# Merged weight words of block 0: from PSUM banks to a buffer in SBUF

## The chip, the cores and the metric

The kernel runs on one core of one Trainium2 chip. The metric is the device time of one execution in microseconds (us). Before the change it is 1144.56 us, the median of 3 runs (1143.82 to 1144.73).

Engines are named as in the profile: PE is TensorE's matmul side and PEld its weight load, DVE is VectorE, ACT is ScalarE, POOL is GpSimd, SP is the queue that issues the DMAs.

## The reference

`x` is 4 x 4096 x 192, `weight_gen` 4 x 4096 x 8 x 7, `w_in` 192 x 2048, `w_out` 2048 x 192, all fp32.

```python
w = softmax(weight_gen)                      # over the last axis, 7 taps
x_pad = concat(zeros(B, 6, D), x)            # causal, along the sequence
out[b, s, h, :] = sum_k w[b, s, h, k] * x_pad[b, s + k, h, :]   # 8 heads of 24
h = out.reshape(16384, 192) @ w_in
g = where(h >= 1, h, where(h <= -1, 0, (h + 1)**2 / 4))
return g @ w_out                             # 16384 x 192
```

## The kernel before

The 16384 tokens are cut into 32 blocks of 512. For each block the dynamic convolution runs on POOL (7 products and 6 sums of 128 x 768, lines 171 to 202), the result is transposed, and two matmuls follow: gemm1 (192 to 2048, line 378) and gemm2 (2048 to 192, line 432). To keep fp32 accuracy each operand is split into a high part in TensorE's fp32r form and a low rest: gemm1 has three passes (high x high, low weight x high, high weight x low) over three pieces of the contraction, 9 passes on each of two row halves, 18 matmuls for a pair of hidden chunks. gemm2 has 32 matmuls for a pair. A block has 16 steps (hidden chunks of 128), that is 8 pairs; there are 256 pairs in all. Between gemm1 and gemm2 stand, for each step, relu and square on ACT (lines 389 and 392), act_g on DVE (397), and the split into gh on ACT (403) and gl on DVE (404).

The order on every engine is the order in which the program is written (`manual_schedule`): each engine takes its instructions one by one. The loop over pairs w (line 676) writes gemm1 of pair w, then gemm2 of pair w - 2, then the elementwise work of pair w; `side` holds work for other blocks that is put into places of this loop.

Block 0 is special: while its pairs run, the weights are decoded, one chunk c (of 8) ahead of the pair that uses it. A chunk has two parts, part 0 for `w_in` and part 1 for `w_out`. For each part:

- cast: the top halves of the raw words go to a 16-bit head, on ACT (`cast_act`, line 327) or DVE (`cast_dve`, line 331);
- `merge(c, part)` (line 340, DVE): a shift-and-or of two SBUF operands, 128 x 384 words, makes the value that the fp32r copy is to see; its output `psw` is a tile of the PSUM pool `ps_h`;
- `high(c, part)` (line 352, ACT): copies `psw` to whi or wo;
- `low(c, part)` (line 356, DVE): `psw` less the high part, into wlo or the low half of wo.

`ps_h` has four banks under one tag. In block 0 they are shared by the two `psh` tiles of gemm1 of a pair, by the two `psw` tiles of a chunk, and by the `psx` tiles of the transposes of blocks 0 and 1. A tile takes the bank that was freed first; so gemm1 of pair w writes the banks that low(w, 0) and low(w, 1) have just freed, and its first two matmuls wait for these two instructions.

`early_pair(w)` (line 631) writes for pairs 2 to 6: merge(c, 0), merge(c, 1) with c = w + 1, one operation of block 1's convolution on POOL, relu of step 2w, high(c, 0), high(c, 1), low(c, 0), low(c, 1), square, relu, square, act_g, the next chunk's cast on DVE, a second operation on POOL, act_g, the splits, the next chunk's cast on ACT. `first_pairs` (line 589) does the same for pairs 0 and 1 and chunks 1 and 2, with one softmax product (line 155) and three convolution products on POOL behind merges. In block 0 each POOL operation has an added dependency (`held`, line 191) on the last merge or cast on DVE that is written ahead of it ("the decoding of a chunk goes first"). After chunk 7 POOL has the last two sums of block 1's convolution; their result is copied in part by ACT (`again`), transposed on TensorE (`turn1`), split by ACT and DVE (`edge_pair`, line 656), and is what gemm1 of pair 8, the first of block 1, needs.

`XT` is the SBUF tile (128 x 3 x 4 x 128 fp32, one buffer) into which the transposed rows of a block are gathered by DMA, from block 2 on (`transpose_out`, line 271). Block 2's gather is the first to write it.

Of the kernel before, what the change touches and what calls it, by code (L numbers as in the profile page):

```python
# [10 lines left out]
F32 = mybir.dt.float32  # L11
# [11 lines left out]
def kernel(  # L23
# [22 lines left out]
    P = 128  # L46
# [33 lines left out]
    xt = ctx.enter_context(tc.tile_pool(name="xt", bufs=2))  # L80
# [5 lines left out]
    ps_h = ctx.enter_context(tc.tile_pool(name="ps_h", bufs=4, space=bass.MemoryType.PSUM))  # L86
# [211 lines left out]
    C1 = NC * P  # L298
# [31 lines left out]
        o, i = tops(c, part)  # L330
        marks.append(nc.vector.tensor_scalar(out=o, in0=i, scalar1=0.5, scalar2=None, op0=ALU.mult))  # L331

    psw = {}

    def merge(c, part):
        word = raw_t[c].bitcast(U32)[:, 1:1 + 2 * CN].rearrange("p (c t) -> p c t", t=2)[:, :, 0]
        upper = heads[c % 2].rearrange("p c t -> p (c t)").bitcast(U32)
        psw[c, part] = ps_h.tile([P, 512], F32, tag="h", name="psw")
        sl = (slice(0, C1), slice(C1, CN))[part]
        marks.append(nc.vector.scalar_tensor_tensor(  # L340
            out=psw[c, part].bitcast(U32)[:, 0:sl.stop - sl.start], in0=word[:, sl], scalar=13, in1=upper[:, sl],
            op0=ALU.logical_shift_right, op1=ALU.bitwise_or))
# [190 lines left out]
    with tc.manual_schedule():  # L533
# [31 lines left out]
        for k, t in enumerate(pieces):  # L565
            for c in range(NC):
                turn_sum(src, t, k == 0, k == len(pieces) - 1, c)
        merge(0, 0)
        cast_dve(0, 1)
        high(0, 0)  # L570
        run(s1[4:6])
        low(0, 0)
        run(split_x(0, src, [nc.vector] * NC))
        cast_dve(1, 2)
        merge(1, 0)
        turned1 = whole()
        n_ops = conv(1, nc.gpsimd, marks, turned1)
# [10 lines left out]

        def first_pairs():
            merge(0, 1)  # L590
            merge(1, 1)
            tc.add_manual_dep(s1[6]().ins, marks[-1].ins.name, SYNC, reason="the decoding of a chunk goes first")
# [159 lines left out]
```

## Time and profile before

| what | value |
|---|---|
| median of 3 runs | 1144.56 us (1143.82 to 1144.73) |
| the profiled execution, its own time | 1144.88 us |
| its span | 1142.4 us |
| PE busy | 1128.4 us (99%) |
| PEld busy | 1112.8 us (97%) |
| ACT busy | 964.5 us (84%) |
| DVE busy | 834.3 us (73%) |
| POOL busy | 792.4 us (69%) |
| mean granted TensorE clock | 0.997 |
| chain that ended last | PE 96% (gemm1 49%, gemm2 46%) |

Times in the rows are counted from the span's start. The span is what the profile covers of the execution; the execution's own time is 2.5 us longer. Busy shares are means over the whole span; block 0, which the change touches, takes the first 60 us of it, and for that stretch the rows by window and the instruction lists are read instead. In an instruction list "x2" means two instructions of one kind in a row, and an entry in brackets the idle time before it and what ended it.

### The profile page before, as it was taken

The page shows a single profiled execution, that of the slowest core. Times are in us where ns is not written, and L with a number is a line of the kernel's source. Part 1 is how long each engine was busy: PE and PEld are TensorE (multiplying, and loading weights), DVE is VectorE, ACT ScalarE, POOL GpSimd, SP SyncE. Part 2 cuts the span into 40 slices and gives each one's busy share as a digit, 9 for nine tenths or more (in the row PEclk, how much of TensorE's full clock was granted, in tenths as well). Part 3 has the DMA queues.
Part 4 walks back from the last instruction along what each step waited for, and adds up shares of the span by engine and source line. Part 5 has one row for each costly group of instructions (what it writes and reads, how often), then busy time and mean ns, then how long its engine had stood idle before and what let it go on. Part 6 is the DMA issues. An engine that isn't in the chain of part 4 may idle for free.

```text
span 1142.4 us, 32241 instructions
## 1 busy us (share of the span) xinstructions
PE 1128.4 (99%) x12885; PEld 1112.8 (97%) x12885; DVE 834.3 (73%) x1271; ACT 964.5 (84%) x1745; POOL 792.4 (69%) x511
## 2 busy tenths in 40 slices
PE   7999999999999999999999999999999999999998
PEld 5889999999999999999999999999999999999998
DVE  8887867777676777767777677776767777677765
ACT  6878888888888888888888888888888888888886
POOL 4699876777857678486686866778576785866310
PEclk9899999999999999999999999999999999999999
DMA  9512222222222122222122222222222122221100
GB/s 230 116 67 83 92 85 92 72 64 79 90 78 91 59 74 89 73 96 90 44 90 73 86 91 78 65 73 90 77 92 72 61 91 82 81 91 43 48 24 29
DMA packets 84053, 91.43 MB, mean 80 GB/s; under 512 B 5056, under 2 KB 75712, under 8 KB 83904
## 3 DMA queue, kind: packets, MB, share of 16 engines
q1 hardware_dynamic: 83904, 89.39, 24.6%
q8 instruction: 101, 1.65, 0.6%
q14 instruction: 48, 0.39, 0.1%
HBM read 64.99 MB, written 24.38 MB: 78 GB/s over the span
## 4 chain that ended last, share of the span: by engine, by line
PE 96%; ACT 1%; DVE 1%; DMA 0%; POOL 0%; issue 0%; SPq 0%; DVEq 0%; POOLq 0%
PE psh L378 49%; PE o L432 46%; PE psx L267 1%; DMA x<-in_x_dram 0%; ACT u L392 0%; ACT u L389 0%; ACT gh L403 0%; DVE psh L397 0%; DVE psw L340 0%; ACT whi L352 0%; POOL piece L189 0%; POOL acc L189 0%; ACT wo L352 0%; DVE gl L404 0%; DVE wo L356 0%
## 5 line engine op out<-in xcount | busy, mean ns | idle before, releaser
L432 PE MATMUL o<-wo,gh 64*128 64x384 f32 x4096 | 638.3, 353 | 1.0 <-SPq L441 1.0
L432 PE MATMUL o<-wo,gl 64*128 64x192 f32 x4096 | 615.1, 247 | 0.0
L432 PEld LDWEIGHTS o<-wo,gh 64*128 64x128 f32 x4096 | 609.3, 184 | 2.4 <-SPq L441 1.2
L432 PEld LDWEIGHTS o<-wo,gl 64*128 64x128 f32 x4096 | 591.3, 188 | 0.7
L397 DVE SCALAR_TENSOR_TENSOR psh<-u,psh 128x512 f32<-128x512 f32 x512 | 354.4, 695 | 282.2 <-ACT u L392 281.8
L378 PE MATMUL psh<-hc,whi 64*128 64x512 f32 x1536 | 436.6, 396 | 3.6 <-DVE wlo L356 2.5
L378 PE MATMUL psh<-hc,wlo 64*128 64x512 f32 x1536 | 430.5, 389 | 0.0
L378 PE MATMUL psh<-hl,whi 64*128 64x512 f32 x1536 | 429.5, 388 | 0.0
L389 ACT ACTIVATE u<-psh 128x512 f32<-128x512 f32 x512 | 301.4, 589 | 79.0 <-PE psh L378 77.8
L404 DVE TENSOR_TENSOR gl<-psh,gh 128x512 fp32r<-128x512 f32 x512 | 345.2, 684 | 15.5 <-ACT gh L403 1.1
L403 ACT ACTIVATE gh<-psh 128x512 fp32r<-128x512 f32 x512 | 299.0, 591 | 64.7 <-DVE psh L397 64.7
L189 POOL TENSOR_TENSOR acc<-acc,pr 128x768 f32<-128x768 f32 x185 | 343.4, 1856 | 6.5 <-DVE head L331 2.8
L392 ACT ACTIVATE u<-u 128x512 f32<-128x512 f32 x512 | 324.3, 633 | 16.0
L179 POOL TENSOR_TENSOR pr<-x,w 128x768 f32<-128x768 f32 x186 | 286.6, 1548 | 7.0 <-DVE psw L340 7.0
L378 PEld LDWEIGHTS psh<-hc,whi 64*128 64x128 f32 x1536 | 270.6, 185 | 8.7 <-DVE wlo L356 3.9
L378 PEld LDWEIGHTS psh<-hl,whi 64*128 64x128 f32 x1536 | 270.5, 185 | 3.1 <-DVE hl L259 0.3
L378 PEld LDWEIGHTS psh<-hc,wlo 64*128 64x128 f32 x1536 | 270.9, 186 | 1.6
L259 POOL TENSOR_TENSOR hl<-XT,hc 128x512 fp32r<-128x512 f32 x90 | 115.8, 1303 | 206.9 <-PE o L432 151.6
L179 POOL TENSOR_TENSOR acc<-x,w 128x768 f32<-128x768 f32 x31 | 47.9, 1546 | 70.2 <-DVE w L155 68.3
L258 ACT ACTIVATE hc<-XT 128x512 fp32r<-128x512 f32 x90 | 55.5, 618 | 0.0
L284 DVE STREAM_TRANSPOSE T<-acc 128x768 f32<-128x768 f32 x30 | 50.2, 1672 | 0.0
L457 DVE SCALAR_TENSOR_TENSOR osb<-o,osb 128x384 f32<-128x384 f32 x64 | 32.5, 548 | 2.8 <-ACT osb L456 2.8
(44 smaller groups left out, 188.8 us busy)
## 6 DMA issues: line engine op xcount, KB each, us to landing
x<-in_x_dram SPq DMA_DIRECT2D x28, 960.0 KB, 5.0
XT<-D SPq DMA_DIRECT2D x180, 128.0 KB, 2.7
out_dram<-osb SPq DMA_DIRECT2D x31, 384.0 KB, 3.1
D<-T SPq DMA_DIRECT2D x30, 384.0 KB, 2.3
x<-in_x_dram SPq DMA_DIRECT2D x4, 945.0 KB
w<-in_weight_gen_dram SPq DMA_DIRECT2D x15, 224.0 KB, 2.6
r<-in_moe_w_in_dram SPq DMA_DIRECT2D x16, 192.0 KB, 7.3
r<-in_moe_w_out_dram SPq DMA_DIRECT2D x8, 384.0 KB, 12.5
```

What stands on the lines that cost most here:

```text
L179: held(eng.tensor_tensor(out=t, in0=xtile[:, k:k + n, :].rearrange("p j (h g) -> p j h g", h=H), in1=wt[:, gi, :, :, k:k + 1].to_broadcast ...
L189: held(eng.tensor_tensor(out=o, in0=s, in1=t, op=ALU.add))
L258: ops.append(lambda c=c: nc.scalar.activation(out=hc[:, c], in_=src[c], func=AF.Copy))
L259: ops.append(lambda c=c: lows.append(engines[c].tensor_tensor(out=hl[:, c], in0=src[c], in1=hc[:, c].bitcast(F32), op=ALU.subtract)))
L284: lambda: nc.vector.transpose(out=T.rearrange("p b c j -> p b j c"), in_=acc.rearrange("p j (r b) -> p b j r", b=R)),
L378: nc.tensor.matmul(out=pair[h][:, 0:N], lhsT=l[rows, f // 2, (c + h) % NC if b < 2 else c], rhs=r[rows, c], start=(s == 0), stop=(s == len ...
L389: nc.scalar.activation(out=u_t[i], in_=h_t[i][:, 0:N], func=AF.Relu, scale=0.5 * UNIT, bias=0.5)
L392: nc.scalar.activation(out=u_t[i], in_=u_t[i], func=AF.Square, scale=UNIT ** -0.5)
L397: nc.vector.scalar_tensor_tensor(out=pv, in0=uv, scalar=1.0 / UNIT, in1=pv, op0=ALU.min, op1=ALU.max)
L403: nc.scalar.activation(out=gh[:, 0:N], in_=gv, func=AF.Copy)
L404: nc.vector.tensor_tensor(out=gl[:, 0:N], in0=gv, in1=gh[:, 0:N].bitcast(F32), op=ALU.subtract)
L432: mm = nc.tensor.matmul(out=o_t[b][turn][:, k, 0:cols], lhsT=g_t[i][l][rows, t * P:(t + 1) * P], rhs=wo[rows, f].rearrange("p s d -> p (s ...
```

## The change

The words that merge makes no longer stand in PSUM. One SBUF tile of four quarters (128 x 4 x 384 fp32) is taken from the buffer `XT`, which is not in use before block 2; a chunk's part takes the quarter 2 * part + c % 2. The PSUM banks of `ps_h` are left to `psh` and `psx`. Who writes and reads the words stays: merge on DVE writes, high on ACT and low on DVE read. The order of the instructions stays too.

```diff
-    psw = {}
+    psw, words = {}, []
 
     def merge(c, part):
         word = raw_t[c].bitcast(U32)[:, 1:1 + 2 * CN].rearrange("p (c t) -> p c t", t=2)[:, :, 0]
         upper = heads[c % 2].rearrange("p c t -> p (c t)").bitcast(U32)
-        psw[c, part] = ps_h.tile([P, 512], F32, tag="h", name="psw")
+        if not words:
+            words.append(xt.tile([P, 4, C1], F32, tag="XT", name="words", bufs=1))
+        psw[c, part] = words[0][:, 2 * part + c % 2]
         sl = (slice(0, C1), slice(C1, CN))[part]
         marks.append(nc.vector.scalar_tensor_tensor(
             out=psw[c, part].bitcast(U32)[:, 0:sl.stop - sl.start], in0=word[:, sl], scalar=13, in1=upper[:, sl],
```

## Rows read from the trace of the kernel before

**Rows 1.** Busy us (and instructions) by stretch; PEclk is the granted clock's share.
```profile
core 0: us, PE busy (x) PEld busy (x) DVE busy (x) ACT busy (x) POOL busy (x), PEclk, DMA share, GB/s
12.00:60.00 48.00, 42.49 (x380) 35.21 (x380) 42.85 (x80) 40.30 (x79) 27.75 (x18) 0.93 0.68 156
...
60.00:1135.00 1075.00, 1075.00 (x12428) 1069.79 (x12428) 780.36 (x1176) 919.25 (x1656) 757.09 (x481) 1.00 0.23 76
```

**Rows 2.** Chain of waits in order of time: start us, us, what.
```profile
30.16 4.57 PE psh L378 x18
...
59.99 2.07 PE psh L378 x18
62.05 2.25 PE o L432 x32
```

**Rows 3.** ScalarE's instructions, pair 4: start us, us, what, idle before.
```profile
39.87 0.60 ACT L389 ACTIVATE u<-psh 128x512 f32<-128x512 f32 x1 [0.49 <-PE psh L378]
```

**Rows 4.** VectorE's instructions from chunk 6's merges to chunk 7's.
```profile
44.89 1.02 DVE L340 SCALAR_TENSOR_TENSOR psw<-r,head 128x384 uint32<-128x384 uint32 x2
46.01 0.56 DVE L356 TENSOR_TENSOR wlo<-psw,whi 128x384 fp32r<-128x384 f32 x1
46.48 0.55 DVE L356 TENSOR_TENSOR wo<-psw,wo 128x384 fp32r<-128x384 f32 x1
...
48.75 1.45 DVE L404 TENSOR_TENSOR gl<-psh,gh 128x512 fp32r<-128x512 f32 x2
50.11 1.02 DVE L340 SCALAR_TENSOR_TENSOR psw<-r,head 128x384 uint32<-128x384 uint32 x2
```

**Rows 5.** POOL's instructions, pair 5 to the end of block 1's convolution.
```profile
46.06 1.55 POOL L179 TENSOR_TENSOR pr<-x,w 128x768 f32<-128x768 f32 x1 [1.33 <-DVE psw L340]
...
51.28 1.83 POOL L189 TENSOR_TENSOR acc<-acc,pr 128x768 f32<-128x768 f32 x1 [1.37 <-ACT whi L352]
53.19 1.85 POOL L189 TENSOR_TENSOR piece<-acc,pr 128x768 f32<-128x768 f32 x1
```

**Rows 6.** All engines in order of time, 114 to 118 us.
```profile
114.20 1.56 POOL L179 TENSOR_TENSOR pr<-x,w 128x768 f32<-128x768 f32 x1
...
114.56 1.68 DVE L150 TENSOR_TENSOR w<-w,m 128x448 f32<-128x448 f32 x1
...
115.70 2.25 POOL L189 TENSOR_TENSOR acc<-acc,pr 128x768 f32<-128x768 f32 x1
```

**Rows 7.** Two lines of the softmax: ns min/median/max over the trace, forms.
```profile
L150 DVE TENSOR_TENSOR w<-w,m x16: 381/615/1676, 3.2 to 1014.2; 128x448 f32<-128x448 f32 x14, 128x224 f32<-128x224 f32 x2
...
L153 DVE TENSOR_SCALAR s<-s x17: 185/904/1801, 5.0 to 1028.1; 128x64 f32<-128x64 f32 x15, 128x32 f32<-128x32 f32 x2
```

**Rows 8.** All engines in order of time, chunks 1 to 3.
```profile
18.88 0.55 DVE L356 TENSOR_TENSOR wlo<-psw,whi 128x384 fp32r<-128x384 f32 x1
...
19.11 0.98 POOL L155 TENSOR_TENSOR w<-w,s 128x448 f32<-128x448 f32 x1 [7.11 <-DVE psw L340]
...
19.55 1.02 DVE L356 TENSOR_TENSOR wo<-psw,wo 128x384 fp32r<-128x384 f32 x2
...
21.92 1.54 POOL L179 TENSOR_TENSOR acc<-x,w 128x768 f32<-128x768 f32 x1 [1.83 <-DVE psw L340]
...
22.77 0.54 DVE L356 TENSOR_TENSOR wo<-psw,wo 128x384 fp32r<-128x384 f32 x1
...
23.42 3.05 POOL L179 TENSOR_TENSOR pr<-x,w 128x768 f32<-128x768 f32 x2
...
28.42 0.57 DVE L340 SCALAR_TENSOR_TENSOR psw<-r,head 128x384 uint32<-128x384 uint32 x1
```

**Rows 9.** ScalarE's groups by form, hc: busy us, mean ns, idle before.
```profile
L258 ACT ACTIVATE hc<-XT 128x512 fp32r<-128x512 f32 x90 | 55.5, 618 | 0.0
...
L258 ACT ACTIVATE hc<-psx 128x512 fp32r<-128x512 f32 x6 | 3.2, 594 | 0.4 <-PE psx L267 0.3
```

**Rows 10.** Busy us by stretch, columns as in rows 1, around the low clock.
```profile
26.80:30.16 3.36, 1.42 (x18) 1.17 (x17) 3.20 (x8) 2.81 (x7) 0.63 (x1) 0.94 1.11 209
29.74:36.57 6.83, 6.41 (x35) 5.48 (x37) 5.81 (x12) 5.60 (x12) 4.72 (x3) 0.50 1.11 216
```

## The prediction

> **What bounds the kernel now.** Read the stretches by engine first [rows 1]: from 60 to 1135 us TensorE is busy 1075.00 of 1075.00 us at the full clock, so nothing done there by another engine is worth anything, and any delay of the point where this stretch begins is a delay of the end, one for one. The change touches only block 0, which is over at 60 us. In 12 to 60 TensorE has 5.5 us of idle and runs below full clock, while VectorE and ScalarE are busy 43 and 40 of 48 us; so the question is what decides when TensorE's closed stretch begins, at 59.8 us.
>
> The chain of waits [rows 2] shows it: it goes through TensorE only where the clock was low (4.57 us for the 18 matmuls of pair 3, against 2.07 for the same 18 at 59.99), otherwise it hops between VectorE and ScalarE. One pair on VectorE [rows 4]: two merges at T = 44.89, two low() at 46.01 and 46.48, two act_g, a cast, two gl from 48.75, and the next merges at 50.11. That is 5.22 us with hardly a gap. Four such intervals from merge(3,0) at 28.42 to merge(7,0) at 50.11 make 5.42 each [rows 4, 8]. Beside it POOL runs block 1's conv, each operation released by a merge or a cast [rows 5]: the product at 46.06 lasts 1.55 us and lies across both low().
>
> **What the change removes.** The first pass of gemm1_pair(w) no longer takes the banks that low(w, 0) and low(w, 1) free, so it can start behind high(w, 0). That is worth at most one low() per pair (0.55 us) and only where TensorE is late. ScalarE waited 0.49 us for gemm1 of pair 4 at 39.87 [rows 3]; in pairs 5 and 6 it didn't wait for TensorE at all. So the gain is at most 0.5 us, and nothing if something else gets later. I take 0.
>
> **Durations of the moved operands.** high() now reads SBUF: hc from XT takes 618 ns, from PSUM 594, at 512 columns [rows 9], so 0.02 to 0.04 us more; one of them lies on the path in each of seven chunks, +0.2 us. merge() and low() on VectorE: a sum of two SBUF operands takes 615 ns at 448 columns and 381 at 224 [rows 7], that is 1.04 ns a column and 0.55 us at 384, which is what low() takes now with one operand in PSUM [rows 4]. So 0 there. SP's queue gets no new instruction; a weight load waits for the merges four chunks ahead of its own, so it shifts as they do and stays as far ahead of its use.
> [...]
>
> **What the change adds: low() reads two SBUF operands.** The case in the trace that decides is a TENSOR_TENSOR on VectorE with both operands in SBUF while POOL works [rows 6]: POOL's product runs 114.20 to 115.76; VectorE's operation began at 114.56 and took 1.68 us, ending at 116.24, 0.48 behind POOL. The same operation takes 0.615 in the median [rows 7]. POOL's next one then took 2.25 in place of 1.85 and ended 1.71 behind VectorE's. So one waits for the other, in turn, and who waited ends at the other's end plus its own duration less 0.13. low() of today, with one operand in PSUM, takes its 0.55 under POOL's product without any stretch [rows 4, 5].
> [...]
>
> So a low() ends 0.42 us after POOL's operation, a product (1.55) 1.42 and an add (1.85) 1.72 after VectorE's. Four terms.
>
> *Chunks 0 and 1* [rows 8]. low(1,0) runs from 18.88 to 19.43 and holds POOL's softmax product: this one, ready at 19.11 (0.98), ends at 19.43 + 0.85 = 20.28; low(0,1) ends at 20.70 where it ended at 20.10. VectorE has no idle there: **+0.6**.
>
> *Chunk 2* [rows 8]. Behind merge(2,1) POOL has three products queued, the first from 21.92, now 22.52 to 24.07. low(2,0) waits for it: ends 24.49. Product 2 is waiting then and goes next, to 25.91; low(2,1) ends at 26.33 instead of 23.32, 3.0 later. Before merge(3,0) lie three act_g, four gl and a cast, 7 x 0.60 + 0.29 = 4.5 us with some 0.2 of waiting (5.1 in the trace, which held 0.5 of idle that is gone, since ScalarE has caught up): merge(3,0) at 31.0, not 28.42. So 2.6 in all, **+2.0** beyond the first term.
>
> *Pairs 2 to 5.* From T: low(c,0) T+1.14 to T+1.69, just ahead of POOL's product (T+1.17, as 46.01 against 46.06); POOL goes next, to T+3.11; low(c,1) to T+3.53; then act_g, cast, act_g and gl (2.1), a wait of 0.1 for gh, gl (0.6): next merge at T+6.27 against 5.42. If POOL comes first, the two low() end at T+3.6, which is the same. 4 x 0.85 = **+3.4**.
>
> *Chunk 7* [rows 5]. POOL's last two operations are adds and the end of block 0 hangs on them. Before: 53.19 + 1.85 - 50.11 = T+4.93. Now low(7,0) to 1.70, add to 3.42, low(7,1) to 3.84, last add to 5.56: **+0.6**. From there again(), the transposes and the split are what they were.
>
> Sum 6.6, with the 0.2 of high() 6.8 us.
>
> **TensorE's clock.** [...] I take a fifth, 0.6 us. Low end 0, high end 3.4.
>
> **The sum.** The profiled execution took 1144.88 us (span 1142.4), 0.3 above the median of 1144.56. 1144.88 + 6.8 + 0.6 = 1152.3; against the median 1152.0 us.
>
> **Rivals.**
> [...]
> 2. The clock falls in the last idle: 6.8 + 3.4 to 4: 1155 us. For it: gemm1 of pair 7 is done near T+3.8 and the transposes start behind the last add and again(), near T+6.1, an idle of 2.3 us. Against: before the end it fell only once in the trace, and about as long an idle is then spread over every pair.
> 3. The other side: low() isn't blocked, because what blocked at 114.56 was the broadcast operand or the softmax's layout, not the second SBUF operand. Then only the freed banks count: gemm1 of pair 3, at 30.16, starts one low() earlier, behind high(); pairs 3 and 4 move up by 0.55, of which ScalarE's wait of 0.49 lets 0.5 through [rows 2, 3]: 1144.1 us, up to 0.7 less if the low clock is missed too. The point that decides is whether low() keeps 0.55 us under a POOL operation. [...]
> 4. The change doesn't free what it says, since the words' buffer makes a new wait: merge(c+2) into the same quarter, or block 2's gather into XT. Neither is late: low(c) is ahead of merge(c+2) on VectorE itself, and block 2's gather is written into the order six turns of the pair loop behind low(7,1). Price 0, so it only joins rival 3.
>
> **Chances.** The forecast 0.55, rival 1 0.17, rival 2 0.18, rivals 3 and 4 0.10. A difference under 0.2% (2.3 us) can't be told from none. Forecast, rivals 1 and 2 are slower by more: 0.89 with a little of rival 1's low end taken off; same 0.09; faster 0.02. The range leaves out rival 3 and the far end of rival 2: 1147.5 to 1156.5 us.
>
> **What would show it.** low() (L356) with a mean over 1 us, the longest 1.5 or more, each ending some 0.4 us behind a POOL operation; POOL's products in block 0 at over 1.9; the merges of chunk 7 at about 56 us and the closed stretch of TensorE from about 67; high() at 0.51. [...] The prediction is wrong if low() stays at 0.55 under POOL, or if the stretch up to the merges of chunk 7 grows by less than 3 us.

## The result, and the profile after

The changed kernel takes 1151.3 us in the median of six runs (1149.89 to 1152.16), the kernel before beside it 1144.29: a ratio of 1.0055 [1.004, 1.007]. That is slower by 0.55%, as forecast, 0.7 us under the predicted time and inside its range. The profiled execution took 1150.63 us with a span of 1148.8, against 1144.88 and 1142.4.

Busy time by stretch, after, answers to [rows 1]:

```profile
core 0: us, PE busy (x) PEld busy (x) DVE busy (x) ACT busy (x) POOL busy (x), PEclk, DMA share, GB/s
12.00:66.00 54.00, 41.11 (x373) 32.86 (x373) 51.01 (x79) 40.77 (x79) 29.55 (x18) 0.94 0.61 139
...
32.90:39.73 6.83, 5.91 (x34) 5.12 (x36) 6.08 (x10) 4.84 (x10) 3.84 (x3) 0.50 0.87 173
...
66.00:1141.00 1075.00, 1075.00 (x12428) 1069.77 (x12427) 780.94 (x1175) 919.34 (x1657) 757.33 (x481) 1.00 0.23 76
```

The closed stretch of TensorE is the same 1075 us with the same 12428 matmuls; it begins 6 us later. The clock's half stretch lies at 32.9 to 39.7, where it began at 29.7. In front of the closed stretch ScalarE does the same 79 instructions in the same 40 us, and VectorE is busy 51.0 us for 79 instructions where it was 42.9 for 80. With no instruction added, the 8.2 us more are time in which the engine stands inside an instruction. Which one, the groups of instructions say (ns min/median/max of the eight of each part, first and last start):

```profile
L358 DVE TENSOR_TENSOR wlo<-words,whi x8: 494/558/1916, 14.1 to 57.1; 128x384 fp32r<-128x384 f32 x8
L358 DVE TENSOR_TENSOR wo<-words,wo x8: 545/1474/2201, 19.3 to 57.5; 128x384 fp32r<-128x384 f32 x8
```

L358 is low(), L356 before (the lines behind merge() stand two further down). Eight of its sixteen instances keep their 0.49 to 0.56 us; the others take 1.05 to 2.20, and the mean of all is 1.15. What holds them stands on POOL. VectorE, chunks 2 and 3, then from chunk 6's merges to the end of chunk 7 (start, us), as [rows 4, 8]:

```profile
20.98 1.01 DVE L342 SCALAR_TENSOR_TENSOR words<-r,head 128x384 uint32<-128x384 uint32 x2
22.50 1.69 DVE L358 TENSOR_TENSOR wlo<-words,whi 128x384 fp32r<-128x384 f32 x1
24.12 1.90 DVE L358 TENSOR_TENSOR wo<-words,wo 128x384 fp32r<-128x384 f32 x1
...
30.71 1.02 DVE L342 SCALAR_TENSOR_TENSOR words<-r,head 128x384 uint32<-128x384 uint32 x2
...
49.64 1.02 DVE L342 SCALAR_TENSOR_TENSOR words<-r,head 128x384 uint32<-128x384 uint32 x2
50.78 0.56 DVE L358 TENSOR_TENSOR wlo<-words,whi 128x384 fp32r<-128x384 f32 x1
51.25 1.90 DVE L358 TENSOR_TENSOR wo<-words,wo 128x384 fp32r<-128x384 f32 x1
...
55.92 1.02 DVE L342 SCALAR_TENSOR_TENSOR words<-r,head 128x384 uint32<-128x384 uint32 x2
...
57.53 2.20 DVE L358 TENSOR_TENSOR wo<-words,wo 128x384 fp32r<-128x384 f32 x1
```

and POOL beside it, as [rows 5]:

```profile
18.74 1.16 POOL L155 TENSOR_TENSOR w<-w,s 128x448 f32<-128x448 f32 x1 [7.08 <-DVE words L342]
...
22.24 1.54 POOL L179 TENSOR_TENSOR acc<-x,w 128x768 f32<-128x768 f32 x1 [2.34 <-DMA x<-in_x_dram]
23.74 3.67 POOL L179 TENSOR_TENSOR pr<-x,w 128x768 f32<-128x768 f32 x2
...
50.80 1.94 POOL L179 TENSOR_TENSOR pr<-x,w 128x768 f32<-128x768 f32 x1 [1.10 <-DVE words L342]
...
57.08 2.24 POOL L189 TENSOR_TENSOR acc<-acc,pr 128x768 f32<-128x768 f32 x1 [1.10 <-ACT whi L354]
59.40 2.01 POOL L189 TENSOR_TENSOR piece<-acc,pr 128x768 f32<-128x768 f32 x1
```

Pair 6 shows the turns. low(6,0) starts at 50.78, 0.02 us ahead of POOL's product, and keeps its 0.56. The product takes 1.94 where it took 1.55 and ends at 52.74; low(6,1), issued at 51.25, ends at 53.15, 0.41 behind it. In chunk 2 POOL's product has begun at 22.24 before low(2,0), and low(2,0) ends at 24.19, 0.41 behind its end; the next product, the first of the two in the row of 23.74, goes before low(2,1) and ends at 25.60, and low(2,1) ends only at 26.02. All eight stretched low() of this trace end 0.41 to 0.42 behind the end of a POOL operation.

The chain of waits now (start, us), as [rows 2]:

```profile
31.85 1.93 DVE wlo L358
...
33.82 3.83 PE psh L380 x12
...
38.68 1.44 DVE wlo L358
...
51.34 1.61 DVE wo L358
...
57.61 1.62 DVE wo L358
...
66.37 2.08 PE psh L380 x18
```

In every chunk from 3 on a stretched low() is a link of the chain: in chunks 3 and 4, where POOL's product had begun first, it is low(c,0), from chunk 5 on low(c,1). The same 18 matmuls that open the closed stretch begin at 66.37 instead of 59.99.

### The profile page after: what moved, and what is told of

It is laid out like the page before. It is cut to its first block, busy times and chain, and to the rows that moved or that the text cites. A ratio compares the mean times of both kernels' runs of the same rounds, so it can differ in the third digit from the quotient of the medians.

```text
span 1148.8 us, 32234 instructions
## 1 busy us (share of the span) xinstructions
PE 1127.7 (98%) x12885; PEld 1111.1 (97%) x12885; DVE 843.7 (73%) x1271; ACT 965.5 (84%) x1745; POOL 794.4 (69%) x511
## 4 chain that ended last, share of the span: by engine, by line
PE 95%; DVE 3%; ACT 1%; issue 0%; DMA 0%; DVEq 0%; SPq 0%
PE psh L380 49%; PE o L434 46%; DVE wo L358 1%; PE psx L267 1%; DVE wlo L358 1%; DVE psh L399 1%; ACT gh L405 0%; DVE words L342 0%; DMA w<-in_weight_gen_dram 0%; ACT whi L354 0%; ACT u L391 0%; DVE head L331 0%; DVE gl L406 0%; DVE piece L227 0%; DVE s L153 0%
## 5 line engine op out<-in xcount | busy, mean ns | idle before, releaser
L434 PEld LDWEIGHTS o<-wo,gh 64*128 64x128 f32 x4096 | 602.6, 184 | 2.5 <-DVE gl L406 1.3
L380 PE MATMUL psh<-hc,whi 64*128 64x512 f32 x1536 | 424.8, 396 | 6.4 <-ACT whi L354 6.4
L380 PE MATMUL psh<-hc,wlo 64*128 64x512 f32 x1536 | 420.3, 390 | 3.5 <-DVE wlo L358 3.3
L380 PE MATMUL psh<-hl,whi 64*128 64x512 f32 x1536 | 419.2, 388 | 0.0
L380 PEld LDWEIGHTS psh<-hc,whi 64*128 64x128 f32 x1536 | 261.5, 185 | 10.2 <-ACT whi L354 7.9
L380 PEld LDWEIGHTS psh<-hc,wlo 64*128 64x128 f32 x1536 | 262.2, 186 | 7.1 <-DVE wlo L358 5.1
L380 PEld LDWEIGHTS psh<-hl,whi 64*128 64x128 f32 x1536 | 261.3, 185 | 3.0 <-DVE hl L259 0.3
```

The source lines that it names most:

```text
L380: nc.tensor.matmul(out=pair[h][:, 0:N], lhsT=l[rows, f // 2, (c + h) % NC if b < 2 else c], rhs=r[rows, c], start=(s == 0), stop=(s == len ...
L434: mm = nc.tensor.matmul(out=o_t[b][turn][:, k, 0:cols], lhsT=g_t[i][l][rows, t * P:(t + 1) * P], rhs=wo[rows, f].rearrange("p s d -> p (s ...
```

## The experiments

Two measures are taken from every profile. "Block 0" is the time from the start of low(1,0) to the first matmul of pair 8: 40.94 us before, 47.70 after; it leaves out the arrival of the first transfers. "Last interval" is from chunk 6's merges to chunk 7's: 5.22 before, 6.28 after; no trace has a stretch of half clock in it (granted clock 1.00 from 36.57 to 60.00 before, from 39.73 to 66.00 after). Times are medians, but of one execution each where a kernel was run once more; the kernel before beside them lay at 1143.9 to 1144.3.

| kernel | time, us | block 0, us | last interval, us |
|---|---|---|---|
| before / after | 1144.3 / 1151.3 | 40.94 / 47.70 | 5.22 / 6.28 |
| part 0's words alone in SBUF, two traces | 1146.41; 1147.66 | 42.28; 42.75 | 5.23; 5.22 |
| part 1's words alone in SBUF, two traces | 1147.6; 1146.41 | 43.49; 43.47 | 5.89; 5.89 |
| POOL held behind both low() | 1148.38 | 45.70 | 5.97 |
| the same, and the cast ahead | 1147.89 | 46.08 | 5.59 |
| POOL only writes: after / before | 1143.45 / 1143.3 | 40.38 / 40.18 | 5.24 / 5.22 |
| POOL in halves: after / before | 1148.18 / 1144.0 | 44.64 / 40.36 | 5.76 / 5.23 |
| after, once more | 1152.16 | 48.90 | 6.28 |

Block 0 isn't free of the clock. In the trace before, half clock from 29.7 to 36.6 us (0.50 in [rows 10]) lengthened two intervals, by 0.8 us in all. And from the end of POOL's last add to pair 8 it takes 4.8 us in every trace in which POOL does the convolution, except three with half clock in just this stretch: POOL held (5.7 us, half clock from 59.4 to 62.8; mean granted clock of the execution 0.998), the same with the cast ahead (5.7; 60.5 to 63.9; 0.995) and the changed kernel once more (6.2; 63.4 to 66.8; 0.995).

**Half of the change: part 0's words, or part 1's.** Part 1's differs in the number alone.

```diff
-        psw[c, part] = words[0][:, 2 * part + c % 2]
+        psw[c, part] = words[0][:, 2 * part + c % 2] if part == 0 else ps_h.tile([P, 512], F32, tag="h", name="psw")
```

> Words of part 0 (w_in) alone stand in SBUF, those of part 1 are back in PSUM. Theory (low() with two SBUF operands and POOL's operation wait for each other in turn): low(c,0) mostly starts just ahead of POOL's operation, so it keeps 0.55 us in most chunks and POOL's product is stretched instead (1.9 us); low(c,1), in PSUM, is never stretched. So about 1.1 us over the kernel before, near 1145.4 (1144.5 to 1147). Rival A (a word in SBUF costs by itself, whoever else works): half of the whole change's 6.4, near 1147.5, with low(c,0) long in every chunk. Rival B (what costs is that gemm1 runs into other banks): the same as the whole change as soon as a bank is freed, near 1150.

> Words of part 1 (w_out) alone stand in SBUF, those of part 0 are back in PSUM. Theory: low(c,1) comes when POOL's operation is running in every chunk, ends 0.42 behind it (about 1.4 us long), low(c,0) keeps 0.55. About 3.6 us over the kernel before, near 1147.9 (1146.8 to 1149): three times as much as with part 0 alone. Rival A: the same as part 0 alone, near 1147.5. Rival B: the same as part 0 alone, near 1150.

Part 0's: 1146.41 us (1145.59 to 1154.57), 1.0026 [1.0014, 1.0038]; block 0 +1.34. Part 1's: 1147.6 us, 1.0028 [1.0017, 1.0039]; block 0 +2.55. The low() of the part that stayed in PSUM keeps 0.55 us in both, and the one with two SBUF operands is the one that waits (it takes up to 1.92 us for part 0, 1.80 for part 1). But part 1 costs about twice part 0 by block 0, not three times; the two intervals of the ratio overlap, so the times alone don't tell the halves apart. The longest of the first runs of part 0, which is the one that was traced, had something else in it (last section). So both were run once more.

> Words of part 0 alone in SBUF once more, for a trace without the 6.9 us that VectorE stood at 117 us in the first one. Theory: 1 to 1.6 us more than the kernel before between low(1,0) and pair 8; the softmax subtraction at 117 us waits for one POOL operation (1.5 to 1.8 us) as in the other traces, or again for all that POOL has queued.

> Words of part 1 alone in SBUF once more, for a trace without the late first transfers of the first one. Theory: 2.5 to 3.5 us more than the kernel before between low(1,0) and pair 8, low(c,0) at 0.55 and low(c,1) at 1.4 to 1.5 in every chunk from 3 on.

Part 0 again: 1147.66 us, block 0 +1.81, somewhat over the 1 to 1.6 expected; part 1 again: 1146.41, +2.53, with low(c,1) at 1.44 to 1.51 in chunks 3 to 6 and at 1.80 in chunk 7, where POOL's operation is an add. VectorE with part 1 alone, chunk 6:

```profile
46.60 0.55 DVE L342 SCALAR_TENSOR_TENSOR words<-r,head 128x384 uint32<-128x384 uint32 x1
47.25 0.56 DVE L358 TENSOR_TENSOR wlo<-psw,whi 128x384 fp32r<-128x384 f32 x1
47.74 1.51 DVE L358 TENSOR_TENSOR wo<-words,wo 128x384 fp32r<-128x384 f32 x1
```

POOL beside it:

```profile
47.30 1.54 POOL L179 TENSOR_TENSOR pr<-x,w 128x768 f32<-128x768 f32 x1 [1.09 <-DVE words L342]
```

The product lies across both low(). It neither holds nor is held by the first, which reads PSUM, and keeps 1.54 us; the second ends 0.41 behind it. Now part 0 alone, VectorE in chunks 3 and 6:

```profile
29.84 1.92 DVE L358 TENSOR_TENSOR wlo<-words,whi 128x384 fp32r<-128x384 f32 x1
31.68 0.55 DVE L358 TENSOR_TENSOR wo<-psw,wo 128x384 fp32r<-128x384 f32 x1
...
47.70 0.56 DVE L358 TENSOR_TENSOR wlo<-words,whi 128x384 fp32r<-128x384 f32 x1
...
49.26 0.65 DVE L331 TENSOR_SCALAR head<-r 128x384 f16<-128x384 bf16 x1
```

and POOL:

```profile
29.80 1.54 POOL L179 TENSOR_TENSOR pr<-x,w 128x768 f32<-128x768 f32 x1 [1.90 <-DVE psw L342]
...
47.73 1.94 POOL L179 TENSOR_TENSOR pr<-x,w 128x768 f32<-128x768 f32 x1 [1.10 <-DVE psw L342]
```

Here a lead of 0.03 us decides. In chunk 6 low() is ahead (47.70 against 47.73): POOL waits, its product ends at 49.67, the cast waits a little (0.65 for 0.38), and the interval is 5.22 us, as before the change. In chunk 3 POOL is ahead (29.80 against 29.84) and low() takes 1.92; that interval is 6.29 in both traces of this kernel. This lost start alone lengthens one interval by 1.07, where 1.1 us had been expected for all of block 0. The waiting cast costs nothing here. The second trace has one more long interval, 6.36 behind chunk 4's merges, which begins at half clock (mean of this execution 0.997) and has a low(4,0) of 0.96, behind 1.14 us of waiting for high().

The two halves don't add up to the whole: 3.9 to 4.3 us against 6.76 by block 0. That gap is too wide, because the 0.8 us of half clock in the trace before is taken off each half; by the medians it is 2.2 + 3.4 against 7.0. The last interval, free of the clock, shows it best: 0.01 for part 0 and 0.67 for part 1, but 1.06 for both. The rows say why: with part 1 alone low(c,1) waits 0.96 us (1.51 - 0.55), because the product had started unhindered. With both, the first low() pushes the product back by 0.4 and the second low() waits for the pushed product, 1.35 (1.90 - 0.55). A conflict that costs nothing by itself makes the next one longer, here by 0.39.

**POOL held behind both low().** POOL's first operation of a chunk is written behind low(c,1) and waits for it, so that neither low() can meet one.

```diff
-        nc.vector.tensor_tensor(out=lo, in0=src, in1=hi.bitcast(F32), op=ALU.subtract)
+        marks.append(nc.vector.tensor_tensor(out=lo, in0=src, in1=hi.bitcast(F32), op=ALU.subtract))
...
-            wave(1)
             if c + 4 < NCH:
...
             low(c, 1)
+            wave(1)
```

> The changed kernel with POOL's first operation of a chunk (three in chunk 2) written behind both low() and made to wait for the second one, not for the second merge. Theory: every low() is back at 0.55 us, but POOL's product now lies over the cast on DVE, which waits for it (over 1 us), and the following add runs into the next merges; about 1.6 us less than the changed kernel, 4.7 over before, near 1149.1 (1147.5 to 1150.5). Rival A: low() as long as in the changed kernel (mean 1.15 us), and later POOL work: 1151 or more. Rival B: as the changed kernel, 1151.

Measured 1148.38 us, 1.004 [1.0028, 1.0052]; block 0 45.70. VectorE in chunk 6:

```profile
47.71 0.56 DVE L358 TENSOR_TENSOR wlo<-words,whi 128x384 fp32r<-128x384 f32 x1
48.18 0.55 DVE L358 TENSOR_TENSOR wo<-words,wo 128x384 fp32r<-128x384 f32 x1
...
49.30 1.37 DVE L331 TENSOR_SCALAR head<-r 128x384 f16<-128x384 bf16 x1
```

POOL:

```profile
48.88 1.55 POOL L179 TENSOR_TENSOR pr<-x,w 128x768 f32<-128x768 f32 x1 [2.24 <-DVE wo L358]
```

Both low() are back at 0.55, and so is every other but low(0,1), which still meets the softmax product (1.05). The wait has moved to the cast: 1.37 us, ending 0.24 behind the product. Here VectorE goes first with both low() and the cast then waits, at an interval of 5.97; left to themselves, the two engines didn't take turns that way. Of the 45.70 some 0.9 us is the clock just before pair 8 (see above).

**The same, with the cast in front.** As the last, and the cast goes behind the merges, where POOL is still in its add.

```diff
             merge(c, 1)
-            wave(1)
+            if c + 1 < NCH:
+                cast_dve(c + 1, 1)
...
             low(c, 1)
+            wave(1)
...
-            if c + 1 < NCH:
-                cast_dve(c + 1, 1)
```

> As the kernel that holds POOL behind both low(), and the cast on DVE is written ahead of them, behind the merges, so that POOL's two operations of a chunk follow each other and only the next chunk's first merge can wait. Theory: low() 0.55, cast 0.38, one merge of a chunk stretched; about 3.3 us over before, near 1147.6 (1146.3 to 1149), 1.4 less than with the cast where it was. Rival A: no less than the changed kernel. Rival B: as the changed kernel, 1151.

Measured 1147.89 us, 1.0035 [1.0023, 1.0047]. VectorE:

```profile
47.09 1.36 DVE L342 SCALAR_TENSOR_TENSOR words<-r,head 128x384 uint32<-128x384 uint32 x2
...
52.68 0.89 DVE L342 SCALAR_TENSOR_TENSOR words<-r,head 128x384 uint32<-128x384 uint32 x1
```

and POOL's add, under which the merge of 52.68 begins:

```profile
51.30 1.85 POOL L189 TENSOR_TENSOR acc<-acc,pr 128x768 f32<-128x768 f32 x1
```

The casts are at 0.38 and both low() at 0.55. Now the first merge, which reads two SBUF operands too, takes 0.89 instead of 0.55, ending 0.42 behind the add. The last interval is 0.4 shorter than with the gate alone, yet block 0 is no shorter, 46.08 against 45.70, and the medians differ by 0.5 us where 1.4 was expected. Both traces lost 0.9 us to the clock just before pair 8, so that isn't the difference. But in this one the clock was at half from 29.8 to 36.6 us as well (mean granted clock 0.995, where it was 0.998 with the gate alone), and the first two intervals took 6.58 and 6.06 where the last two took 5.6; how much of that is the clock was not separated. In all three places that were tried for POOL's work in this loop, some VectorE instruction with SBUF operands meets it (a low() of 1.90 us, a cast of 1.37, a merge of 0.89).

**POOL only writes.** POOL's 13 products and sums of block 1 become memsets of the same tiles under the same gates, in the changed kernel and in the one before. Shown is the cut at the sums; the products have the same.

```diff
-            held(eng.tensor_tensor(out=o, in0=s, in1=t, op=ALU.add))
+            if gate:
+                held(eng.memset(o, 0.0))
+            else:
+                eng.tensor_tensor(out=o, in0=s, in1=t, op=ALU.add)
```

> The changed kernel with POOL's 13 operations of block 1's convolution replaced by memsets of the same tiles, which write SBUF and read nothing (block 1's convolution is left out, its softmax product on POOL stays). Theory (the conflict is over reads): low() is back at 0.55 us from chunk 2 on; only the softmax product still holds low(0,1) of chunks 0 and 1 (0.5 us). So within 0.3 to 1.2 us of the kernel before with the same memsets, near 1144.6. Rival A (a word in SBUF costs by itself): 6 us over the kernel before with the same memsets, low() with a mean of 1.15. If a POOL write alone conflicts too, low(c,1) is stretched by up to the memset's length, some 2 us in all.

> The kernel before with the same memsets in place of POOL's 13 operations of block 1's convolution (left out in the same way). All theories: the kernel's VectorE and ScalarE chain in block 0 stays, POOL's last two operations are shorter, so 0.2 to 1 us below the kernel before, near 1143.8. It is the base for the changed kernel with memsets.

Measured 1143.45 us for the changed kernel, 1.000 [0.999, 1.001] of the unedited kernel before, and 1143.3 for the other, 0.9993 [0.9984, 1.0001]. The 6.8 us are gone but for 0.15 us in the medians and 0.2 in block 0, less than the expected 0.3 to 1.2. The 0.2 is made of 0.56 that low(0,1) still waits for the softmax product (1.05 us), 0.03 in an interval (5.25 against 5.22), and some 0.5 the other way, which the second kernel's trace lost to half clock (16 matmuls of gemm1 took 3.86 us at 30.55, and two intervals 5.39 and 5.56 for 5.22). VectorE in the changed one (low() is L364 there):

```profile
46.03 0.56 DVE L364 TENSOR_TENSOR wlo<-words,whi 128x384 fp32r<-128x384 f32 x1
46.51 0.56 DVE L364 TENSOR_TENSOR wo<-words,wo 128x384 fp32r<-128x384 f32 x1
...
47.63 0.40 DVE L337 TENSOR_SCALAR head<-r 128x384 f16<-128x384 bf16 x1
```

and POOL:

```profile
45.97 0.74 POOL L180 MEMSET pr<- 128x768 f32 x1 [2.34 <-DVE words L348]
```

low() starts under POOL's memset and takes its 0.56, where one under the product took 1.90. So words in SBUF cost next to nothing by themselves, 0.15 us in the medians, which rules out every explanation by their place alone (longer instructions, a wait for the buffer, the order on the engines), and a memset, the one POOL instruction here that only writes SBUF, holds nobody: in these runs the conflict comes with POOL's reads.

**POOL in halves.** Each of the 13 operations is cut into two of 128x384, in both kernels. Shown is the cut at the sums; the products have the same.

```diff
-            held(eng.tensor_tensor(out=o, in0=s, in1=t, op=ALU.add))
+            for j in parts:
+                held(eng.tensor_tensor(out=o[:, j], in0=s[:, j], in1=t[:, j], op=ALU.add))
```

> The changed kernel with each of POOL's 13 operations of block 1's convolution cut into two of half the columns (128x384). Theory: a low() waits for one POOL instruction, now about 0.9 us long, so no low() is over 1.5 us (1.9 to 2.2 before the cut) and the intervals between merges shrink from 6.3 to about 5.8: 2.9 us less than the changed kernel, near 1148.4 (1147 to 1150). Rival A: the length of POOL's instructions doesn't matter, 1151. Rival B: 1151.

> The kernel before with the same cut of POOL's operations. All theories: no low() is stretched; POOL's two operations of a chunk get 0.2 us longer each and the last adds end later: 0.3 us over the kernel before (0 to 1), near 1144.6. It is the base for the cut in the changed kernel.

Measured 1148.18 us, 1.0038 [1.0026, 1.005], and 1144.0, 1.0001 [0.9992, 1.001]. VectorE in the changed kernel (low() is L361):

```profile
47.97 0.56 DVE L361 TENSOR_TENSOR wlo<-words,whi 128x384 fp32r<-128x384 f32 x1
48.44 1.22 DVE L361 TENSOR_TENSOR wo<-words,wo 128x384 fp32r<-128x384 f32 x1
```

and POOL:

```profile
47.99 2.40 POOL L180 TENSOR_TENSOR pr<-x,w 128x384 f32<-128x384 f32 x2 [1.03 <-DVE words L345]
```

low(6,1) now ends at 49.66, inside POOL's two halves (47.99 to 50.39): it goes in between them and waits for one half instead of the whole, 0.67 us instead of 1.35. Halving POOL's instructions takes 3.1 of the 6.8 us away, at no cost to the kernel before, whose low() doesn't wait at all. The price of the change thus goes with the length of the other engine's instruction.

**The changed kernel once more.**

> The changed kernel once more, for a second trace. Theory: from low(1,0) to the first matmul of pair 8 it takes 47.7 us as in the first trace (40.9 in the kernel before), give or take 0.7 with where TensorE's clock falls; of two low() of a chunk one is stretched, by one POOL operation. Rival: the clock carries a good part of the loss; then a trace with the clock elsewhere differs by 2 us or more in that stretch.

1152.16 us, block 0 48.90, 1.2 more than in the first trace: outside the 0.7 that was allowed, and short of the rival's 2. Again one low() of each chunk from 3 on is stretched, and the last interval is the same 6.28; the difference is at the end of block 0, where it takes 6.2 us from POOL's last add to pair 8 instead of 4.8. Busy time by stretch in this second trace:

```profile
core 0: us, PE busy (x) PEld busy (x) DVE busy (x) ACT busy (x) POOL busy (x), PEclk, DMA share, GB/s
60.00:68.00 8.00, 5.92 (x46) 4.84 (x46) 5.61 (x10) 5.64 (x11) 8.00 (x5) 0.79 0.00 0
63.40:66.80 3.40, 3.40 (x21) 2.81 (x20) 2.48 (x4) 2.03 (x5) 3.40 (x3) 0.50 0.00 0
```

From 63.4 to 66.8 the clock was at half (0.50), and in this stretch lie the last gemm2 and transposes on which pair 8 waits. In the first trace it was at full speed there and had fallen from 32.9 to 39.7, inside block 0, where ScalarE once waited 0.75 us for gemm1 and the intervals stayed at 6.29 to 6.35.

No variant that does all of the work beat the kernel before. The only part of the change that can gain, the freed banks, stays under the 0.5 us of the prediction: with POOL's reads gone from block 1's convolution the changed kernel isn't faster than the kernel before edited in the same way.

## Why the prediction was right

Step by step, in its own terms. All of the changed trace up to chunk 1 lies 0.37 us earlier, since the first x transfer landed earlier (POOL's wait for it ended at 7.11 us, before at 7.46); this is taken out below.

| step | forecast | measured |
|---|---|---|
| chunks 0 and 1: merge(2,0) later by | 0.6 | 20.98 for 20.76: 0.59 |
| chunk 2: merge(3,0) later by, in all | 2.6 | 30.71 for 28.42: 2.66 |
| interval of pairs 2 to 5 | 6.27 for 5.42 | 6.30; four make 3.5 |
| merges of chunk 7 at | about 56 | 55.92 |
| chunk 7: POOL's last add ends, from its merges | 5.56 for 4.93 | 5.49 |
| high() | 0.51 | 0.51 to 0.53 |
| mean of low(), longest | over 1, 1.5 or more | 1.15, 2.20 |
| low(1,0) to pair 8 | +6.8 | +6.76 |

**What carried it.** One stretched instruction elsewhere in the trace [rows 6], together with the observation that today's low() is not stretched [rows 4, 5], gave the rule (two SBUF operands wait, in turn, and end 0.42 behind) and the price. All eight stretched low() end 0.41 to 0.42 behind a POOL operation, as forecast. The merges and low() themselves are as long as they were (0.550 us for a merge that writes SBUF, 0.559 before). So the trace shows 9 ns less for a merge and nothing for a low() that doesn't wait.

**The interval's 0.88 is two things.** Free of half clock the interval went from 5.22 to 6.29, 1.07 more. Before, the stretch of half clock made two intervals 5.84 and 5.41, 0.8 us lost; after, a fall of the same 6.83 us cost next to nothing, since TensorE had idle to spare: it was busy 5.91 us of it, where it was 6.41 before. 4 x 1.07 - 0.8 = 3.5. The forecast set its 6.27 against a mean that half clock had lengthened and came out right, since the fall inside block 0 cost next to nothing, but the conflict alone is dearer than its 0.85.

**Where the sum was lucky.** 6.8 against 6.76 is closer than the working deserves. The addends of the interval, 3.53 + 2.1 + 0.1 + 0.6, make 6.33 as they stand and not 6.27, and high()'s 0.02 was in its T+1.14 already, so the 0.2 added for high() at the end counts it a second time for most chunks. The four terms, forecast at 6.6, measured 0.59 + 2.07 + 3.52 + 0.56 = 6.74 with high() in them; the extra 0.2 happened to fill what they were short of. A fifth of 3.4 for the clock is 0.7, not 0.6.

**Where the numbers part.** The profiled execution was forecast at 1152.3 and took 1150.63. The 1.65 us between are: 0.6 for the clock at the end of block 0, which this execution didn't spend; 0.37 for the early start; 0.04 in block 0; and 0.65 outside the span (1.83 us there, 2.48 before; 1.86 in the second trace of the changed kernel). The last stays unexplained. The clock term was the author's estimate, a fifth of a high end of 3.4, and no run shows a loss of either size. What the runs show is a matter of chance: the second trace lost 1.4 us at the end of block 0, the first nothing, and the runs lie between 1149.9 and 1152.2. The high end was too high: where the clock fell in the last idle it cost 0.9 to 1.4 us (POOL held, the same with the cast ahead, the changed kernel once more), and each of these stretches of half clock is 3.4 us long, where the one in [rows 10] took 6.83.

**The rivals.** As in the sum, POOL got its turn between two low() that stood in a row (50.80 between 50.78 and 51.25); VectorE went first with both only where POOL was held back by hand. Rival 3 fell with low() at 1.90 and with a cast without broadcast that took 1.37 us for 0.38 under POOL's product, and the gain that it named doesn't show even where nothing blocks: with memsets an interval is 5.25 against 5.22. Its bound of 0.5 us passed over ScalarE's wait for gemm1 of pair 3, 0.92 us at 34.45 in the trace before. Rival 4 shows nothing: high() and low() wait for no new transfer. Rival 2 came true in one of two traces as to the place of the fall, but at 1.4 us instead of 3.4 to 4.

## What to carry to other kernels

Moving one operand of a two-operand VectorE instruction from PSUM to SBUF left its own duration as it was here (0.55 to 0.56 us) and changed whom it waits for: look at what POOL reads at that moment, add the length of that instruction (1.55 us for a product here, 1.85 for an add), and do it in order, because a first, free wait pushes POOL's operation into the next one (0.39 us more here). If the SBUF place is needed, move one of the two parts only (part 0's words, alone, leave the last interval at 5.22 and 5.23 for 5.22), or cut POOL's instructions shorter; moving them in time helped as much here (1148.4 and 1147.9 us against 1148.2 for the halves), but only passed the wait on to the next VectorE instruction. And where the chain goes through an engine that is at half clock, take the price of a conflict from an interval at full clock (1.07 us here, 0.88 by the mean with half clock in it) and add the loss by hand.

## What the runs showed of the hardware that was not expected

**Turns are not always taken.** In one execution, with part 0's words alone in SBUF, the softmax's subtraction at L150 in block 1, an instruction that the change doesn't touch, came to stand under POOL's convolution. VectorE:

```profile
117.10 6.88 DVE L150 TENSOR_TENSOR w<-w,m 128x448 f32<-128x448 f32 x1
```

POOL:

```profile
116.85 1.56 POOL L179 TENSOR_TENSOR pr<-x,w 128x768 f32<-128x768 f32 x1
118.35 1.85 POOL L189 TENSOR_TENSOR acc<-acc,pr 128x768 f32<-128x768 f32 x1
120.15 1.56 POOL L179 TENSOR_TENSOR pr<-x,w 128x768 f32<-128x768 f32 x1
121.65 1.84 POOL L189 TENSOR_TENSOR acc<-acc,pr 128x768 f32<-128x768 f32 x1
```

It waited through all four POOL operations that stood in a row and ended 0.49 behind the last. TensorE then waited 4.0 us for gl, in the stretch that is otherwise closed, and its granted clock was 0.83 over 120 to 140 us; this execution took 1154.57 us where its kernel has 1146.41. In the other twelve traces the same operation, at 114 to 123 us, waited for one POOL operation (1.48 to 1.81 us). What decides who goes next is open. Single executions of other kernels lay 4 to 7 us high as well (the kernel before once 1148.27, POOL only writing once 1150.33); the same cause would fit, but those weren't traced.

**The clock falls in different places from run to run.** Of the changed kernel one trace has half clock from 32.9 to 39.7 us, the other at 25.8 to 29.2, 46.3 to 49.7 and 63.4 to 66.8 (0.92 over 17 to 60, 0.50 in the last), with the same instructions. Of these only the last cost time to speak of, so a forecast can hold the price of a fall, but not its place.
